# Attention and feed-forward kernel: moves of local results cut at multiples of 16 rows, V of most local blocks loaded in one transfer for all heads

## The chip, the cores and the metric

The kernel runs on one core of one Trainium2 chip. The metric is the device time of one execution in microseconds (us). The kernel before took 1079.87 us, the median of 3 runs (1079.04 to 1081.28).

## What is computed

Inputs q, k and v have 8 batches, 8 heads, 576 positions and 64 elements a head. Every head gets two attentions that are added: one over positions pooled by 4 (144 pooled positions, each result repeated 4 times), and a local one in which a position sees only positions less than 4 away. The result x (8 x 576 rows of 512) goes through a normalization and a feed-forward layer with a residual:

```
out_up    = repeat(softmax(q_d @ k_d.T * scale) @ v_d, 4)        # q_d, k_d, v_d: means of 4 positions
out_local = softmax(where(|i - j| < 4, q @ k.T * scale, -1e9)) @ v
x   = out_up + out_local                                          # as rows of 512 = 8 heads x 64
xn  = (x - mean(x)) / sqrt(var(x) + 1e-6) * g_ln
out = x + relu(xn @ w_ch1) @ w_ch2                                # 512 -> 2048 -> 512
```

## The kernel before, in words

All data are float32. The feed-forward products are made of three products of rounded parts each (`lo`, `hi` of the weights, `xh`, `xlo` and `hh`, `hl` of the data), and they are most of TensorE's work. The 4608 rows of x are 36 tiles of 128 rows (`x0` to `x35`), taken two at a time: 18 chunks c of 256 rows. For each chunk and each of 8 pairs p of weight columns, `up` (L996) makes `h`, ScalarE `relu` (L1003) makes `hh`, VectorE `rest` (L1007) makes `hl`, and `down` (L1019) adds into `acc`.

Local attention works on 40 windows (index i, 5 of them a batch). A window holds 116 positions as two blocks (`par`) of 58 results, read from 64 positions each. Windows 0 to 6 (`by_pe`) are turned by TensorE; in windows 7 to 39 q and k arrive as 32 x 32 blocks (`load_blocks`, L419, tiles `qr` and `kr`, 8 transfers each) and VectorE turns them (`turn`, L499). `load_v` (L437) brings V into one of four tiles `vwin`, with one partition half a block. The results of a window stand in `xl`, with the heads of a pair in different partition halves. `move` (L662) carries them by transfers within SBUF to the rows of x that they belong to: a block's 58 rows are one piece, or two where a tile of x ends within them, and each piece is two transfers, one for each head of the pairs.

The rest of a row's way: `load_up` (L865) reads the pooled result, GpSimd adds it to x (`plus`, L896), VectorE takes statistics (L904 to L907), GpSimd the inverse root (L910), VectorE normalizes (`xn`, L914), TensorE turns it (`px`, L923), ScalarE and VectorE split it (`xh` L930, `xlo` L940).

The order of every engine is set before the run by a planner (`Plan`, L23). Each piece of work is a task with an engine, a duration, the tasks it needs, a due time and the buffers it takes and gives. Most tiles come from one pool of 88 units (`u`). `xl` is one of them, and the task of a window's last move gives it back. A task that takes a unit may get one that the planner believes to be free from that time on. The planner lets a task end at its start and duration; its result is there a `lag` later. For the local blocks turned by VectorE the figures are:

```python
    DMA, LAT, W_AHEAD, W_LAG = 0.5, 2.5, 40, 1.5
        vt = add("SP", 2.65, load_v, (last_local.v[i % NVW],), due - 8.0, lag=LAT, kb=360, ahead=AHEAD)
            t = add("SP", 0.76 if by_pe else 1.52, move, outs, due + 1.0, take=() if n in piece else U,
                    give=U if e == len(moves) - 1 else (), lag=LAT, kb=116)
```

All loads, moves and stores are issued by SyncE (SP) in one queue, in the planner's order. Where a task waits on SP, all that stand behind it wait too. Between tasks of TensorE that the planner sees more than 0.4 us apart in the first 150 us of its plan, it puts spare matmuls (L197).

Of the kernel before, what the change touches and what calls it, by code (L numbers as in the profile page):

```python
# [22 lines left out]
class Plan:  # L23
# [14 lines left out]
    def add(self, eng, dur, fn, deps=(), due=0.0, take=(), give=(), lag=None, ahead=1e9, alt=None, kb=0):  # L38

        opts = {eng: (dur, fn, 0.0)}  # L40
        if alt is not None:
            opts[alt[0]] = alt[1:]
        t = SimpleNamespace(
            n=len(self.tasks), opts=opts, dur=dur, deps=[d for d in deps if d is not None],
            due=due, take=take, give=give, lag=lag, ahead=ahead, open=0.0, waits=0, eng=None, fn=None, kb=kb,
        )
        self.tasks.append(t)
        return t
# [91 lines left out]
def attention_then_ffn(  # L140
# [10 lines left out]
    nc = tc.nc  # L151

    P = 128
    B, H, S, D = q.shape
# [19 lines left out]
    NVW = 4  # L174
# [18 lines left out]
    def psa(name):  # L193
        p = ps_a.tile([P, 512], F32, tag="a", name=name)

        for _ in range(warm.pop() if warm else 0):
            nc.tensor.matmul(p[:, :P], lhsT=ident, rhs=ident, start=True, stop=True)  # L197
        return p
# [95 lines left out]
    def window_at(i):  # L294
        if NWIN <= i < NWIN + NEARLY:
            return w_base + i * w_gap - EARLY
        return w_base + i * w_gap if i >= NWIN else norm_at(0) - B0W - B0W_GAP * (2 - i)
# [7 lines left out]
    AHEAD = 45  # L305
# [14 lines left out]
    DMA, LAT, W_AHEAD, W_LAG = 0.5, 2.5, 40, 1.5  # L320
# [4 lines left out]
    def dve(n):  # L325
        return 0.06 + n / 950.0
# [72 lines left out]
    def window_start(w, par):  # L399
        return min(max(NQ * (2 * w + par) - (FACTOR - 1), 0), S - 64)  # L400

    chosen, own_moves = {}, []
    last_local = SimpleNamespace(v=[None] * NVW)

    def local(i):
        b, w = divmod(i, NWIN)
        due = window_at(i)
        add = plan.add
        x = SimpleNamespace(r={}, p={}, raw={})
        vwin = vwins[i % NVW]  # L410
# [21 lines left out]
        def load_v():  # L432
            for par in range(2):
                t0 = window_start(w, par)
                if not by_pe:
                    for h2 in range(2):
                        nc.sync.dma_start(  # L437
                            vwin[64 * par : 64 * par + 64, h2, :, :D],
                            v[b].rearrange("(p h) s d -> h s p d", h=2)[h2, t0 : t0 + 64],
                        )  # L440
                    continue
                for h2 in range(2):
                    nc.sync.dma_start(
                        vwin[64 * h2 : 64 * h2 + 64, par, :, :D],
                        v[b].rearrange("(p h) s d -> h s p d", h=2)[h2, t0 : t0 + 64],
                    )

        turned = []
        by_pe = i < NPE
        own = b < NPB  # L450
        for src, nm in ((q, "q"), (k, "k")):
            if by_pe:
# [15 lines left out]
                def sums(nm=nm):  # L468

                    for par in range(2):  # L470
# [17 lines left out]
                        lag=LAT, kb=360, ahead=AHEAD)  # L488
# [6 lines left out]
            else:  # L495
# [9 lines left out]
                for jb in range(2):  # L505
                    ts.append(add("SP", 4 * DMA, lambda src=src, nm=nm, jb=jb: load_blocks(src, nm, jb), ts,
                                  due - 14.0, take=() if jb else U, lag=LAT, kb=200, ahead=AHEAD))
                turned.append(add("DVE", dve(512), turn, ts, due - 8.0, take=U, give=U))
        vt = add("SP", 2.65, load_v, (last_local.v[i % NVW],), due - 8.0, lag=LAT, kb=360, ahead=AHEAD)

        def scores_by_pair():

# [71 lines left out]
        def times_v():  # L584


            x.pv = [
                psa(f"lv{i}_{n}")[:, : NPAIR * (D + 1)].rearrange("p (h e) -> p h e", h=NPAIR)
                for n in range(2)
            ]  # L590
            for pr in range(NPAIR):
                for n in range(2):
                    js = slice(64 * n, 64 * n + 64)
                    for m in range(2):
                        hs = slice(64 * m, 64 * m + 64)
                        nc.tensor.matmul(  # L596
                            x.pv[n][hs, pr], lhsT=x.at[js, pr, hs], rhs=vwin[js, m, pr], start=True, stop=True
                        )

        def inverse(h2):  # L600
# [24 lines left out]
        t = add("PE", 0.43, turn_a, (t,), due - 3.0, take=A, give=U)  # L625
        at = add("ACT", act(512), turn_a_out, (t,), due - 3.0, take=U, give=A)
        last_local.v[i % NVW] = tv = add("PE", 0.7, times_v, (at, vt), due - 1.0, take=(("a", 2),), give=U)
        outs = []
        for h2 in range(2):
# [6 lines left out]
        for par in range(2):  # L636
            s0 = NQ * (2 * w + par)
            n = min(NQ, S - s0)
            t, r0 = b * S + s0, s0 - window_start(w, par)
            while n:  # L640
                m = min(n, P - t % P)
                moves.append((t // P, t % P, r0, m, par))
                t, r0, n = t + m, r0 + m, n - m
        if own:
# [417 lines left out]
    for i in range(NPB * NWIN):  # L1062
        local(i)
    for b in range(B):
        pooled(b)
    for i in range(NPB * NWIN, B * NWIN):
        local(i)
# [48 lines left out]
```

## Time and profile before

| | kernel before |
|---|---|
| median of 3 runs | 1079.87 us (1079.04 to 1081.28) |
| profiled execution, span from first to last instruction | 1080.9 us |
| TensorE busy | 1040.3 us, 96% of the span |
| VectorE, ScalarE, GpSimd busy | 511.9, 312.7, 266.2 us |
| mean granted TensorE clock | 0.989 |
| bytes moved | 104.34 MB, mean 97 GB/s |

The profiled execution has no other time than its span; the span is 1.0 us above the median of the runs and within their range. TensorE is PE in the rows, VectorE DVE, ScalarE ACT, GpSimd POOL, SyncE's queue SPq; a `q` behind an engine's name is its sequencer. A busy time says that an engine had work, not that the work was at its fastest: at the lower of the clock's two levels the same matmul is busy longer.

### The profile page before, as it was taken

The page shows a single profiled execution, that of the slowest core. Times are in us where ns is not written, and L with a number is a line of the kernel's source. Part 1 is how long each engine was busy: PE and PEld are TensorE (multiplying, and loading weights), DVE is VectorE, ACT ScalarE, POOL GpSimd, SP SyncE. Part 2 cuts the span into 40 slices and gives each one's busy share as a digit, 9 for nine tenths or more (in the row PEclk, how much of TensorE's full clock was granted, in tenths as well). Part 3 has the DMA queues.
Part 4 walks back from the last instruction along what each step waited for, and adds up shares of the span by engine and source line. Part 5 has one row for each costly group of instructions (what it writes and reads, how often), then busy time and mean ns, then how long its engine had stood idle before and what let it go on. Part 6 is the DMA issues. An engine that isn't in the chain of part 4 may idle for free.

```text
span 1080.9 us, 23774 instructions
## 1 busy us (share of the span) xinstructions
PE 1040.3 (96%) x9290; PEld 933.6 (86%) x9290; DVE 511.9 (47%) x1309; ACT 312.7 (29%) x852; POOL 266.2 (25%) x285
## 2 busy tenths in 40 slices
PE   8987999989989999999999999999979999999998
PEld 8875898978879898989898989898968988888997
DVE  7699954434243535345344443645424353543211
ACT  5675633222222322132222221223212222222110
POOL 4234454314004221141213231142311400100000
PEclk9999899989999999999999999999999999999999
DMA  7798554625333443344343435252533333300000
GB/s 155 211 270 235 121 147 112 144 61 120 82 88 89 99 97 79 65 92 107 82 110 77 109 69 125 47 137 51 126 87 76 69 74 74 85 10 30 9 20 20
DMA packets 289296, 104.34 MB, mean 97 GB/s; under 512 B 237945, under 2 KB 276089, under 8 KB 289185
## 3 DMA queue, kind: packets, MB, share of 16 engines
q1 hardware_dynamic: 289185, 102.83, 40.2%
q8 instruction: 73, 1.20, 0.5%
q14 instruction: 38, 0.31, 0.1%
HBM read 82.58 MB, written 11.80 MB: 87 GB/s over the span
## 4 chain that ended last, share of the span: by engine, by line
PE 78%; DMA 9%; DVE 5%; SPq 4%; issue 2%; ACT 1%; POOL 1%; DVEq 0%; ACTq 0%; POOLq 0%
PE h L996 33%; PE acc L1019 32%; PE gv L802 3%; DMA s<-in_moe_w_ch_dram 2%; PE lv L596 2%; PE ls L540 2%; DMA x<-xl 2%; PE gs L766 2%; PE lt L575 1%; SPq L419 1%; PE px L923 1%; PE gt L785 1%; SPq L662 1%; DVE cva L370 1%; SPq L428 1%
## 5 line engine op out<-in xcount | busy, mean ns | idle before, releaser
L1019 PE MATMUL acc<-hi,hl 128*128 128x512 f32 x576 | 239.1, 415 | 10.2 <-DVE hl L1007 8.5
L1019 PE MATMUL acc<-lo,hh 128*128 128x512 f32 x576 | 228.5, 397 | 0.0
L1019 PE MATMUL acc<-hi,hh 128*128 128x512 f32 x576 | 226.8, 394 | 0.0
L1007 DVE SCALAR_TENSOR_TENSOR hl<-h,hh 128x512 fp32r<-128x512 f32 x144 | 98.9, 687 | 242.8 <-ACT hh L1003 222.8
L1003 ACT ACTIVATE hh<-h 128x512 fp32r<-128x512 f32 x144 | 86.1, 598 | 433.5 <-PE h L996 379.7
L996 PE MATMUL h<-xh,lo 128*128 128x256 f32 x1152 | 193.5, 290 | 0.0
L996 PE MATMUL h<-xlo,hi 128*128 128x256 f32 x1152 | 185.6, 284 | 0.0
L996 PE MATMUL h<-xh,hi 128*128 128x256 f32 x1152 | 185.6, 283 | 0.0
L996 PEld LDWEIGHTS h<-xh,lo 128*128 128x128 f32 x1152 | 169.4, 190 | 17.6 <-POOL lo L383 0.2
L996 PEld LDWEIGHTS h<-xlo,hi 128*128 128x128 f32 x1152 | 159.4, 192 | 0.0
L996 PEld LDWEIGHTS h<-xh,hi 128*128 128x128 f32 x1152 | 159.1, 192 | 0.0
L896 POOL TENSOR_TENSOR x<-x,up 128x512 f32<-128x512 f32 x32 | 41.2, 1289 | 376.8 <-DMA x<-xl 264.5
L1019 PEld LDWEIGHTS acc<-hi,hl 128*128 128x128 f32 x576 | 110.1, 191 | 27.5 <-DVE hl L1007 11.4
L1019 PEld LDWEIGHTS acc<-hi,hh 128*128 128x128 f32 x576 | 109.2, 190 | 25.3
L1019 PEld LDWEIGHTS acc<-lo,hh 128*128 128x128 f32 x576 | 110.3, 191 | 12.7
L930 ACT ACTIVATE xh<-px,gain 128x128 fp32r<-128x128 f32 x144 | 44.3, 367 | 79.5 <-PE px L923 43.6
L940 DVE SCALAR_TENSOR_TENSOR xlo<-px,gain,xh 128x128 fp32r<-128x128 f32 x144 | 43.0, 344 | 38.3 <-ACT xh L930 26.1
L904 DVE BATCH_NORM_STATS2 st<-x 128x6 f32<-128x512 f32 x32 | 22.1, 690 | 69.9 <-POOL x L896 68.7
L1027 DVE SCALAR_TENSOR_TENSOR x<-acc,x 128x512 f32<-128x512 f32 x36 | 24.3, 683 | 35.5 <-PE acc L1019 35.3
L546 DVE TENSOR_TENSOR ls<-ls,mask 128x256 f32<-128x256 f32 x66 | 27.0, 424 | 27.3 <-PE ls L540 22.3
L779 ACT ACTIVATE ag<-gs,gmx 96x144 f32<-96x144 f32 x96 | 28.8, 373 | 35.1 <-DVE gmx L771 33.1
L802 PEld LDWEIGHTS gv<-vd,agt 72*72 72x72 f32 x512 | 37.1, 145 | 1.5
(195 smaller groups left out, 1152.7 us busy)
## 6 DMA issues: line engine op xcount, KB each, us to landing
s<-in_moe_w_ch_dram SPq DMA_DIRECT2D x64, 256.0 KB
vwin<-in_v_dram SPq DMA_DIRECT2D x160, 64.0 KB
out_dram<-x SPq DMA_DIRECT2D x36, 256.0 KB
qr<-in_q_dram SPq DMA_DIRECT2D x264, 32.0 KB
kr<-in_k_dram SPq DMA_DIRECT2D x264, 32.0 KB
up<-ud SPq DMA_DIRECT2D x28, 256.0 KB
x<-xl SPq DMA_DIRECT2D x66, 58.0 KB
ud<-od SPq DMA_DIRECT2D x32, 72.0 KB
```

The lines of the kernel that those rows point to most:

```text
L546: nc.vector.tensor_add(x.ps[n], x.ps[n], mask.unsqueeze(1).broadcast_to([P, NPAIR, 64]))
L779: nc.scalar.activation(y.a[:, c], y.ps[:, c], AF.Exp, scale=POOLED_SCALE, bias=y.mx[:, c : c + 1])
L802: nc.tensor.matmul(y.pv[:, qh, h2], lhsT=y.at[kh][:, h2, qh * GH : (qh + 1) * GH], rhs=vd[:, kh, 2 * pr + h2], start=kh == 0, stop=kh == 1,)
L896: nc.gpsimd.tensor_add(xt[n], xt[n], x.up)
L904: nc.vector.bn_stats(st, x.up if by_pe else xt[n])
L930: nc.scalar.activation(xh[c][i][:, k, j * P : (j + 1) * P], pxt[n][:, kc], AF.Copy, scale=gain[:, kc : kc + 1])
L940: nc.vector.scalar_tensor_tensor(out=xlo[c][i][:, k, ts], in0=pxt[n][:, kc], scalar=gain[:, kc : kc + 1], in1=xh[c][i][:, k, ts].bitcast(F ...
L996: nc.tensor.matmul(ph[c, p][:, fi], lhsT=wt[:, kc], rhs=xx[kc // 2][:, kc % 2], start=n == 0, stop=n == 3 * KC - 1)
L1003: nc.scalar.activation(hh[c, p], ph[c, p], AF.Relu)
L1007: nc.vector.scalar_tensor_tensor(out=hl[c, p].rearrange("p c t -> p (c t)"), in0=ph[c, p].rearrange("p c t -> p (c t)"), scalar=0.0, in1=h ...
L1019: nc.tensor.matmul(acc[c][j], lhsT=lt[:, fi, ts], rhs=rt, start=p == 0 and fi == 0 and n == 0, stop=p == NPR - 1 and fi == 1 and n == 2,)
L1027: nc.vector.scalar_tensor_tensor(out=x, in0=acc[c][j], scalar=1.0 + 2.0**-23, in1=x, op0=ALU.mult, op1=ALU.add)
```

## The change

Two things. `load_v` of windows 7 to 39 issues one transfer per block for all 8 heads instead of one for each head of the pairs; so the tile is filled in the order of the heads, and `times_v` (L596) picks its part by another index. The planner's duration for it becomes 1.4 us. And the loop that lists the moves cuts a piece of m rows into the largest multiple of 16 rows and the remainder, for all windows (a remainder below 16 stays whole). Each cut piece is a task of its own with the durations above.

```diff
-                    for h2 in range(2):
-                        nc.sync.dma_start(
-                            vwin[64 * par : 64 * par + 64, h2, :, :D],
-                            v[b].rearrange("(p h) s d -> h s p d", h=2)[h2, t0 : t0 + 64],
-                        )
+                    nc.sync.dma_start(
+                        vwin.rearrange("p a b e -> p (a b) e")[64 * par : 64 * par + 64, :, :D],
+                        v[b, :, t0 : t0 + 64, :].rearrange("h s d -> s h d"),
+                    )
...
-        vt = add("SP", 2.65, load_v, (last_local.v[i % NVW],), due - 8.0, lag=LAT, kb=360, ahead=AHEAD)
+        vt = add("SP", 2.65 if by_pe else 1.4, load_v, (last_local.v[i % NVW],), due - 8.0, lag=LAT, kb=360, ahead=AHEAD)
...
-                            x.pv[n][hs, pr], lhsT=x.at[js, pr, hs], rhs=vwin[js, m, pr], start=True, stop=True
+                            x.pv[n][hs, pr], lhsT=x.at[js, pr, hs], rhs=vwin[js, m, pr] if by_pe else vwin[js, pr // 2, 2 * (pr % 2) + m], start=True, stop=True
...
                 m = min(n, P - t % P)
+                m = m // 16 * 16 or m
                 moves.append((t // P, t % P, r0, m, par))
```

In all, SyncE issues 1257 transfers instead of 1165: 94 loads of V instead of 160, and 350 moves instead of 192 (336 instead of 184 in windows 7 to 39). The planner then orders all engines anew. Three places follow; in the names the number behind a tile's name is its index, the last one a buffer's number, and `64x8x64 x2` means 64 partitions, 8 runs of 64 elements, two transfers in a row.

SyncE's queue at the moves of window 8 (`xl8`), with the loads of windows 10 and 11 (`qr`, `kr`) and of the pooled attention (`raw5`, `raw6`) around them. Before:

```order
L700 DMA raw5v1_3028<-in_v_dram 72x4x256
L419 DMA kr10_3034<-in_k_dram 32x8x32 x4
L419 DMA qr10_2969<-in_q_dram 32x8x32 x4
L825 DMA ud2_2687<-od4_1_3082 72x2x128
L419 DMA kr10_3034<-in_k_dram 32x8x32 x4
L700 DMA raw6q0_3140<-in_q_dram 72x4x256
L700 DMA raw6k0_3143<-in_k_dram 72x4x256
L662 DMA x7_2883<-xl8_3136 58x4x64 x2
L662 DMA x7_2883<-xl8_3136 42x4x64 x2
L662 DMA x8_3175<-xl8_3136 16x4x64 x2
```

Now:

```order
L419 DMA qr10_3004<-in_q_dram 32x8x32 x4
L700 DMA raw5v1_3132<-in_v_dram 72x4x256
L662 DMA x7_2919<-xl8_3128 48x4x64 x2
L662 DMA x7_2919<-xl8_3128 10x4x64 x2
L662 DMA x7_2919<-xl8_3128 32x4x64 x2
L662 DMA x7_2919<-xl8_3128 10x4x64 x2
L662 DMA x8_3200<-xl8_3128 16x4x64 x2
L700 DMA raw6q0_3217<-in_q_dram 72x4x256
L700 DMA raw6k0_3225<-in_k_dram 72x4x256
L436 DMA vwin0_76<-in_v_dram 64x8x64 x2
L419 DMA kr10_3252<-in_k_dram 32x8x32 x4
```

Between `raw5v1` and the moves stood 15 transfers; now there is none, and both halves of `kr10` come behind the moves.

SyncE's queue at the moves of window 31. Before:

```order
L865 DMA up27_10285<-ud6_9047 128x1x512
L419 DMA kr33_10232<-in_k_dram 32x8x32 x4
L437 DMA vwin3_79<-in_v_dram 64x4x64 x4
L662 DMA x27_10126<-xl31_10350 12x4x64 x2
L662 DMA x28_10378<-xl31_10350 46x4x64 x2
L662 DMA x28_10378<-xl31_10350 58x4x64 x2
```

Now:

```order
L865 DMA up27_10372<-ud6_9148 128x1x512
L419 DMA kr33_10392<-in_k_dram 32x8x32 x4
L419 DMA qr33_10367<-in_q_dram 32x8x32 x4
L662 DMA x27_10201<-xl31_10425 12x4x64 x2
L662 DMA x28_10453<-xl31_10425 32x4x64 x2
L662 DMA x28_10453<-xl31_10425 14x4x64 x2
L662 DMA x28_10453<-xl31_10425 48x4x64 x2
L662 DMA x28_10453<-xl31_10425 10x4x64 x2
L419 DMA kr33_10392<-in_k_dram 32x8x32 x4
L436 DMA vwin3_79<-in_v_dram 64x8x64 x2
```

The load of V and the second half of `kr33` have gone behind the moves, the second half of `qr33` stands just ahead of them; the moves are five pieces instead of three.

TensorE at the turn of tile 19 (`px19`), between the last products for chunk 8 (`h8_7` and `acc8`). Before:

```order
L996 MATMUL h8_7_7591<-xlo8_1_6940,hi1_15_2125 128x256 x2
L923 MATMUL px19_7639<-ident_66,xn19_7637 128x128 x4
L1019 MATMUL acc8_0_7240<-hi2_11_1876,hl8_5_7538 128x512
L1019 MATMUL acc8_0_7240<-lo2_11_1888,hh8_5_7505 128x512
L1019 MATMUL acc8_0_7240<-hi2_11_1876,hh8_5_7505 128x512
L1019 MATMUL acc8_1_7241<-hi2_11_1876,hl8_5_7538 128x512
L1019 MATMUL acc8_1_7241<-lo2_11_1888,hh8_5_7505 128x512
L1019 MATMUL acc8_1_7241<-hi2_11_1876,hh8_5_7505 128x512
L739 MATMUL gq10_1_7661<-ident_66,qd10_6945 128x72 x2
```

Now:

```order
L996 MATMUL h8_7_7650<-xlo8_1_6999,hi1_15_2149 128x256 x2
L1019 MATMUL acc8_0_7295<-hi2_11_1896,hl8_5_7595 128x512
L1019 MATMUL acc8_0_7295<-lo2_11_1919,hh8_5_7564 128x512
L1019 MATMUL acc8_0_7295<-hi2_11_1896,hh8_5_7564 128x512
L1019 MATMUL acc8_1_7296<-hi2_11_1896,hl8_5_7595 128x512
L1019 MATMUL acc8_1_7296<-lo2_11_1919,hh8_5_7564 128x512
L1019 MATMUL acc8_1_7296<-hi2_11_1896,hh8_5_7564 128x512
L923 MATMUL px19_7710<-ident_66,xn19_7706 128x128 x4
L739 MATMUL gq10_1_7719<-ident_66,qd10_6806 128x72 x2
```

Six products of `acc8` have gone ahead of `px19`. `px11` and `px29` have moved behind six products in the same way, and `lt9` (the turn of window 9's exponentials) behind six of `acc2`; around `px9` and `px27` the order on TensorE, VectorE and ScalarE is as before.

## Rows read from the trace of the kernel before

**Rows 1.** The page: span, and busy time of TensorE.
```profile
span 1080.9 us, 23774 instructions
PE 1040.3 (96%) x9290; PEld 933.6 (86%) x9290; DVE 511.9 (47%) x1309; ACT 312.7 (29%) x852; POOL 266.2 (25%) x285
```

**Rows 2.** TensorE's waits: line, releaser, total us, times, longest.
```profile
PE px L923 <- DVE xn L914: 13.3, 6, 5.8
```

**Rows 3.** Stretches of 27 us: busy us by engine, granted clock, DMA share, GB/s.
```profile
81.00:108.00 27.00, 19.14 (x166) 15.69 (x166) 26.31 (x47) 15.59 (x42) 13.44 (x11) 1.00 0.82 236
...
216.00:243.00 27.00, 22.01 (x182) 19.26 (x181) 9.26 (x23) 6.24 (x21) 4.24 (x5) 0.87 0.29 61
...
783.00:810.00 27.00, 21.30 (x165) 18.96 (x163) 6.54 (x20) 3.63 (x8) 3.06 (x3) 0.95 0.39 88
810.00:837.00 27.00, 26.92 (x231) 24.31 (x232) 12.79 (x34) 6.87 (x19) 2.77 (x3) 0.92 0.31 75
```

**Rows 4.** ScalarE in order of time at 808 us: start, duration, work, idle before.
```profile
808.30 0.62 ACT L930 ACTIVATE xh<-px,gain 128x128 fp32r<-128x128 f32 x2 [8.93 <-DMA x<-xl]
```

**Rows 5.** Chain that ended last: start, duration, what (three stretches).
```profile
575.55 4.91 DMA x<-xl
...
580.49 0.05 DVEq L940
...
784.53 1.78 DMA qr<-in_q_dram
...
802.83 5.25 DMA x<-xl
...
862.65 4.41 DMA x<-xl
```

**Rows 6.** TensorE's part of that chain: one `down` of two `acc` tiles.
```profile
570.91 1.39 PE acc L1019 x6
```

**Rows 7.** SyncE's queue in order of time, before the moves of window 31.
```profile
793.03 2.06 SPq L419 DMA_DIRECT2D kr<-in_k_dram  x4
795.22 3.14 SPq L437 DMA_DIRECT2D vwin<-in_v_dram  x4
798.46 5.99 SPq L662 DMA_DIRECT2D x<-xl  x6
```

**Rows 8.** SyncE, window 18's second move of 58 rows, and the next one.
```profile
478.19 0.79 SPq L662 DMA_DIRECT2D x<-xl  x1
479.08 1.59 SPq L662 DMA_DIRECT2D x<-xl  x1
```

**Rows 9.** Moves of window 34 (48, then 10 rows), and GpSimd behind them.
```profile
887.00 0.60 SPq L662 DMA_DIRECT2D x<-xl  x1
887.72 0.86 SPq L662 DMA_DIRECT2D x<-xl  x1
889.18 1.30 POOL L896 TENSOR_TENSOR x<-x,up 128x512 f32<-128x512 f32 x1 [24.56 <-DMA x<-xl]
```

**Rows 10.** Issue times of SyncE's lines: count, ns min/median/max, first and last start.
```profile
L662 SPq DMA_DIRECT2D x<-xl x184: 605/787/2176, 194.5 to 1001.6; - x184
L437 SPq DMA_DIRECT2D vwin<-in_v_dram x132: 595/615/1601, 98.5 to 907.7; - x132
L428 SPq DMA_DIRECT2D qn<-in_q_dram x14: 596/634/1471, 1.3 to 53.7; - x14
```

**Rows 11.** SyncE's queue in order of time, at the moves of window 8.
```profile
211.43 2.71 SPq L419 DMA_DIRECT2D kr<-in_k_dram  x4
...
219.49 7.91 SPq L662 DMA_DIRECT2D x<-xl  x6
```

**Rows 12.** VectorE's last work for `xl8`.
```profile
213.47 0.41 DVE L612 TENSOR_TENSOR xl<-lv,lr 128x256 f32<-128x256 f32 x1
```

**Rows 13.** GpSimd's step of the chain behind the moves of window 8.
```profile
227.73 1.30 POOL x L896
```

**Rows 14.** SyncE's waits: line, releaser, total us, times, longest.
```profile
SPq L1033 <- DVE x L1027: 90.1, 16, 38.2
```

## Prediction

> **What bounds the kernel now.** I read the page first: TensorE is busy for 1040.3 of 1080.9 us [rows 1]. Neither part of the change touches a matmul's size or number, apart from a few spare ones, so at most the 40.6 idle us can be won, and what the lower clock costs. Then the waits of TensorE and the stretches of 27 us, to see where the idle time lies. It is not spread. In the first 135 us VectorE is the limit: from 81 to 108 us it is busy for 26.31 of 27 us, and TensorE idles for 7.9 [rows 3]. After 200 us nearly all idle time is a wait of `px` for `xn`: 13.3 us in six waits, the longest 5.8 [rows 2], and one of the six, a short one, lies before 200 us. One more stop, at 230 us, has 27 - 22.01 = 5.0 us [rows 3]. Behind the two long stops the granted clock is below 1: 0.87 from 216 to 243, 0.95 and 0.92 from 783 to 837 us [rows 3]; the clock has two levels, 2.4 and 1.2 GHz, and a mean below 1 is time at the lower. That costs about 27 x 0.13 = 3.5 and 27 x (0.05 + 0.08) = 3.5 us. So 13.3 + 5.0 + 7.0 = 25.3 us are all that can be won outside the start.
>
> The chain of waits tells what stands behind these stops: moves of 58 rows. At 804 us TensorE waits for `px27`, VectorE for an `xlo` ahead of `xn27`, and ScalarE has stood idle for 8.93 us because its `xh` needs a unit that a move still reads; the last of window 31's moves was issued at 802.83 and landed 5.25 us later, and `xh` ran at 808.30 [rows 4, 5]. At 581 us VectorE's own `xlo` waits in the same way for a move that took 4.91, at 867 us for one that took 4.41 [rows 5]. At 230 us it is the sum itself: GpSimd begins `x7` at 227.73, though `xl8` was ready at 213.9 [rows 12, 13].
>
> In all of them the planner was wrong by about the same. It counts 1.52 us for a piece and 2.5 us until it has landed. Window 31's three pieces should take 3 x 1.52 + 2.5 = 7.1 us from the first issue to the last landing; they took from 798.46 to 808.08, 9.6 us [rows 5, 7]. So units were given away, and work was queued, 2.5 us too early.
>
> **The moves.** Two transfers of 58 rows hold up what is issued next: 0.79 us for the second, 1.59 for the one behind it, where 0.79 is usual [rows 8, 10]. A transfer of 48 rows takes 0.60 us to issue, and GpSimd starts on its data 889.18 - 887.00 = 2.2 us after its issue began [rows 9]; a 10-row one takes 0.86 to issue. So a 58-row piece goes from 2 x 0.79 + 0.8 of hold-up to 0.60 x 2 + 0.86 x 2, with a gap of 0.05 behind each: 2.5 before, 3.1 now. What becomes shorter is only the end: 2.2 instead of 4.4 to 5.25 us behind the last issue.
>
> The Trainium skill, in "DMA: Bandwidth & Descriptors" (section "Why a DMA increments its semaphore by 16 and not by 1"), says that a transfer uses as many of 16 engines as the largest number up to 16 that divides its slowest dimension: 2 for 58 rows, 16 for 48, 10 for 10. The trace agrees, as far as it has such rows: 4.4 to 5.25 us against 2.2. By bytes alone 48 rows would take 48/58 of 4.4, or 3.6 us, and the end would gain 0.8 instead of 2 us or more.
>
> Other cuts gain nothing there and only add issues. There are 336 transfers instead of 184 in windows 7 to 39, 10.2 a window instead of 5.6. At the mean of 0.60 and 0.86 with the gap, 0.78, a window takes 7.9 us; window 31 took 5.99 with six and I take 5.6 for the mean [rows 7]. That is +2.3 us a window. For window 31 (12, 32, 14, 48, 10) the last landing is 9 issues x 0.78 + 2.2 = 9.2 us after the first issue, against 9.6. With six pieces, as in 13 windows, it is 11 x 0.78 + 2.2 = 10.8, later than that.
>
> So the moves do not become faster on the whole. But the planner now counts 5 x 1.52 + 2.5 = 10.1 us for what should take 9.2, where it had counted 7.1 for 9.6. It errs to the safe side, and its new order shows it.
>
> **V.** 132 transfers become 66 with the same bytes. Four issues of 0.615 and their gaps are 2.7 us; two, of 0.634 as the loads of `qn` with the same shape take [rows 10], are 1.4: -1.3 us a window. The planner's figures agree with both. The products with V read as many rows as before, from another place of the tile: no cost; I take 0 and at worst 0.1 us a window.
>
> SyncE so issues for 2.3 - 1.3 = 1.0 us more per window, 33 us in all. From below this costs nothing: SyncE waits for the results' stores alone for 90.1 us, 38.2 of it at the end [rows 14]. From above it costs all 33.
>
> **Place by place,** from the new order:
> - 230 us. The moves of window 8 stood behind 15 transfers, issued from 211.43 to 219.49 [rows 11]. Now none stands between `raw5v1` and them, and `xl8` is ready at 213.88 [rows 12]. So they start up to 5.6 us earlier and last as long (9 x 0.78 against 7.9). `lt9`, which waited, also stands behind six products of 1.39 us in all more. The stop and its clock go: 5.0 + 3.5 = 8.5.
> - 804 us. The load of V (3.14 us) and half of `kr33` (2.06) have gone behind the moves [rows 7], so they may start 5.2 us earlier. But `up27`, which must wait for `ud6`, may not come earlier, and behind it there is now half of `qr33` in V's place: then it is 1.1 us. Add 0.4 from the moves themselves; of the stop's 5.8 us I take 4, and the clock's 3.5: 7.5.
> - `px19`, `px11` and `px29` stand behind six products, 1.39 us [rows 6], or two such groups; `px9` has its moves ahead of V. These are the rest of the 13.3: 7.5 us, and I take 7.
>
> The sum is 23.0 us. New stops come against it. Before, six of 33 windows led to one, at 25.3 / 6 = 4.2 us with the clock. The queue is fuller and later loads now stand behind the moves; with errors on the safe side I take half as many, three: +12.6. Its bounds are 0 and 33. At the start the moves of window 5 and some loads for the pooled attention now stand ahead of weights on SyncE, and some `hl` ahead of conversions of weights on VectorE: both signs, I take +0.5, from -4 to +6 (half of the 7.9 idle us [rows 3], or most of it again). So -23.0 + 12.6 + 0.5 = -9.9, and 1080.9 - 9.9 = 1071.0 for the profiled execution; it is 1.0 above the median of the runs, so 1070.0.
>
> **Rivals.**
> 1. *Loads come late instead (slower).* Half of k now stands behind the moves (`kr10`, `kr33`). A block lands about 1.8 us after its issue [rows 5]; behind five pieces (7.8 us) the last of four is issued 9.3 us after the first move and lands 11 us after it. VectorE turns it in a fixed place, and the `xlo` and `hl` behind it wait. Without its stop VectorE would be at `lkt33` some 3 us after the `xh` of [rows 4] less 5.8, at about 805.5 by estimate; so it decides against us where the moves start later than 794.5, and every such window then stops TensorE by the excess. With all 33 us of added issue exposed, against 23 won, it gives 1080 + 10 = 1090. For it: the queue's length; against it: the planner knows the new durations and moved these loads itself.
>
> The Trainium skill speaks for it in the same page ("Rules for kernel authors"): small transfers are mostly overhead and belong together, and here 58 KB become 48 and 10. The trace agrees for the issue: a tenth of the bytes takes 0.86 us.
>
> 2. *The stops only change places.* As many windows as before have one, at other tiles, 23 against 23: 1080. For it: the buffers are as scarce as before, and six-piece windows land later. Against it: the common error of 2.5 us is gone.
>
> 3. *All goes, and the start too.* No new stop, and 4 us at the start: 1079.9 - 23 - 4 = 1053. Against it: the fuller queue, and that the start's limit, VectorE, gets no less to do.
>
> 4. *Cutting does not help a transfer* (48 rows land as 58 do). Then the planner's 2.5 us are short again, with more pieces: 1080 or more. Rows 9 speak against it: 2.2 us. I give it 2%, within rival 2.
>
> **How the numbers follow.** The forecast, most stops gone and a few new ones, 0.57, at 1070, its own range 1060 to 1078; rival 1 0.20; rival 2 0.15; rival 3 0.08. A measurement of this kernel can tell 0.2%, 2.2 us, from no change. Faster by more: nearly all of the forecast (0.55), rival 3 (0.08) and a little of rival 2 (0.02): 0.65. Slower: rival 1 (0.19) and a quarter of rival 2: 0.23. The rest, 0.12, is the same. The range that leaves out 2 in 10 runs from 1056, near rival 3, to 1087, near rival 1.
>
> **What would show it.** Right: the moves of 48 rows issue in 0.6 to 0.7 us, the second of 58 rows no longer delays the next, no `xh` or `xlo` waits for a move, the wait of `px` for `xn` falls below 6 us, and the clock stays at 1 after 200 us. Wrong: `px` waits as long at other tiles; or VectorE's L499 waits for loads of k and TensorE for `hl`; or the start, up to 135 us, has more than 5 us of idle time added. If SyncE's issue time grows by well over 40 us, the moves were under-priced.

## The result, and the profile after

The changed kernel takes 1069.38 us, the median of 4 runs (1068.29 to 1071.13), against 1079.72 (1079.04 to 1081.28) for the one before: a ratio of 0.9898, with a 95% interval of 0.9883 to 0.9913. The forecast was 1070.0. The two profiled executions lie further apart than the medians, 1067.7 and 1080.9 us of span, so that what follows has 13.2 us to explain, of which 10.3 are the change and the rest is the choice of executions: in every run that has both, the device time is 1.7 to 2.3 us above the span, so the profiled execution of before was not 1.0 but some 3 us slower than its median.

The page of the changed kernel, its span and the engines' busy times:

```profile
span 1067.7 us, 24014 instructions
PE 1043.4 (98%) x9318; PEld 937.9 (88%) x9318; DVE 509.0 (48%) x1304; ACT 317.7 (30%) x872; POOL 266.5 (25%) x285
```

TensorE's idle time fell from 40.6 [rows 1] to 24.3 us. Its waits now (line, releaser, total us, times, longest), in which the line of [rows 2] no longer stands at all:

```profile
PE acc L1019 <- DVE hl L1007: 4.6, 3, 2.3
PE gs L766 <- ACT ktg L752: 3.5, 2, 2.8
PE lv L595 <- ACT at L581: 2.7, 1, 2.7
PE lk L457 <- DMA kn<-in_k_dram: 2.5, 2, 1.6
...
PE gv L802 <- POOL mv L910: 1.6, 1, 1.6
```

The stretches of [rows 3] after 200 us, of the changed kernel (TensorE's busy time first, then weight loads, VectorE, ScalarE, GpSimd, granted clock, DMA share, GB/s). From 216 to 243 us the stop and the low clock are gone; the second place still has 2.8 idle us:

```profile
216.00:243.00 27.00, 26.30 (x228) 23.37 (x227) 14.17 (x35) 8.05 (x28) 10.95 (x11) 1.00 0.55 104
...
783.00:810.00 27.00, 24.21 (x176) 21.66 (x174) 8.56 (x21) 6.42 (x20) 3.10 (x3) 0.94 0.39 83
810.00:837.00 27.00, 27.00 (x256) 24.54 (x246) 14.68 (x36) 6.32 (x16) 10.13 (x11) 1.00 0.28 77
```

The same from 200 to 1062 us, of the kernel before:

```profile
200.00:1062.00 862.00, 844.33 (x7465) 758.73 (x7465) 359.48 (x941) 206.18 (x559) 180.83 (x186) 0.99 0.35 80
```

and of the changed kernel; 17.7 idle us became 3.5:

```profile
200.00:1062.00 862.00, 858.51 (x7608) 772.75 (x7604) 359.94 (x943) 215.51 (x592) 183.29 (x188) 1.00 0.37 81
```

Fixed stretches do not hold the same work in both kernels. A mark that stands at the same point of the feed-forward work in both is the n-th `hh` (one for each chunk and pair, 144 in all). These are the 20th and the 24th on ScalarE in order of time (start, duration), of the kernel before:

```profile
210.20 0.60 ACT L1003 ACTIVATE hh<-h 128x512 fp32r<-128x512 f32 x1 [1.93 <-DMA vwin<-in_v_dram]
...
245.36 0.60 ACT L1003 ACTIVATE hh<-h 128x512 fp32r<-128x512 f32 x1 [0.81 <-PE h L996]
```

and of the changed kernel:

```profile
215.18 0.60 ACT L1003 ACTIVATE hh<-h 128x512 fp32r<-128x512 f32 x1 [1.92 <-PE h L996]
...
244.32 0.60 ACT L1003 ACTIVATE hh<-h 128x512 fp32r<-128x512 f32 x1
```

So the changed kernel is 5.0 us behind at the 20th, 1.0 ahead at the 24th, past the first stop, and at the last it is 13.1 ahead (1057.2 against 1070.3): in this pair of executions it wins 18.1 us after the start and loses 5.0 in it.

SyncE, moves of window 18 one by one (48, 48, 10, 10 rows), answering [rows 8]; none of the four is held up:

```profile
469.95 0.64 SPq L662 DMA_DIRECT2D x<-xl  x1
470.64 0.63 SPq L662 DMA_DIRECT2D x<-xl  x1
471.32 0.82 SPq L662 DMA_DIRECT2D x<-xl  x1
472.18 0.79 SPq L662 DMA_DIRECT2D x<-xl  x1
```

At window 31, VectorE's last work for `xl31`, of the kernel before:

```profile
790.16 0.73 DVE L612 TENSOR_TENSOR xl<-lv,lr 128x256 f32<-128x256 f32 x2
```

of the changed kernel:

```profile
782.89 0.73 DVE L611 TENSOR_TENSOR xl<-lv,lr 128x256 f32<-128x256 f32 x2
```

and SyncE's queue of the changed kernel at that place, answering [rows 7]:

```profile
784.99 1.93 SPq L419 DMA_DIRECT2D qr<-in_q_dram  x4
787.01 7.95 SPq L662 DMA_DIRECT2D x<-xl  x10
795.01 2.96 SPq L419 DMA_DIRECT2D kr<-in_k_dram  x4
798.01 1.40 SPq L436 DMA_DIRECT2D vwin<-in_v_dram  x2
```

Before, the moves began 798.46 - 790.89 = 7.6 us after their data were ready; now 787.01 - 783.62 = 3.4. They hold the queue for 7.95 us instead of 5.99, and V for 1.40.

The stop that is left at this place is a new one. The chain that ended last, of the changed kernel, shows it (start, us, what):

```profile
796.02 1.46 SPq L419
...
797.52 1.97 DMA kr<-in_k_dram
...
799.61 0.06 DVE lkt L498
...
800.25 0.58 DVE xlo L940 x2
...
800.85 0.62 ACT xh L930 x2
...
802.25 1.26 PE gs L766 x6
```

The last part of `kr33`, now behind the moves, was issued 10.5 us after the first of them, since the part ahead of it took 1.46 us to issue where the others took 0.44 to 0.47, and landed at 799.49; VectorE waited for it to turn it, with `xlo` behind; `xh`, `ktg` and TensorE's `gs` waited in turn.

### The profile page after: what moved, and what is told of

The parts are those of the page before. It is cut to its first block, busy times and chain, and to the rows that moved or that the text cites. A ratio compares the mean times of both kernels' runs of the same rounds, so it can differ in the third digit from the quotient of the medians.

```text
span 1067.7 us, 24014 instructions
## 1 busy us (share of the span) xinstructions
PE 1043.4 (98%) x9318; PEld 937.9 (88%) x9318; DVE 509.0 (48%) x1304; ACT 317.7 (30%) x872; POOL 266.5 (25%) x285
## 4 chain that ended last, share of the span: by engine, by line
PE 74%; SPq 1%; DMA 1%; DVE 1%; issue 0%; ACT 0%; POOL 0%; POOLq 0%; DVEq 0%
PE h L996 32%; PE acc L1019 31%; PE gv L802 2%; PE lv L595 2%; PE ls L539 2%; PE gs L766 2%; PE lt L574 1%; PE px L923 1%; PE gt L785 1%; SPq L419 1%; SPq L662 1%; DMA kr<-in_k_dram 1%; PE gq L739 0%; DMA x<-xl 0%; DVE x L1027 0%
## 5 line engine op out<-in xcount | busy, mean ns | idle before, releaser
L1019 PEld LDWEIGHTS acc<-lo,hh 128*128 128x128 f32 x576 | 110.0, 191 | 12.6
L802 PE MATMUL gv<-vd,agt 72*72 72x65 f32 x512 | 37.9, 228 | 1.6 <-POOL mv L910 1.6
L910 POOL TENSOR_TENSOR mv<-mv,neg_half 128x1 f32<-128x1 f32 x36 | 19.8, 549 | 77.8 <-DVE mv L907 67.0
```

The source lines that it names most:

```text
L802: nc.tensor.matmul(y.pv[:, qh, h2], lhsT=y.at[kh][:, h2, qh * GH : (qh + 1) * GH], rhs=vd[:, kh, 2 * pr + h2], start=kh == 0, stop=kh == 1,)
L1019: nc.tensor.matmul(acc[c][j], lhsT=lt[:, fi, ts], rhs=rt, start=p == 0 and fi == 0 and n == 0, stop=p == NPR - 1 and fi == 1 and n == 2,)
```

## The experiments

Theory A: the stops came from moves whose hold on SyncE's queue and whose landing the planner counted too short, and they went because the figures now fit. Theory B: they went because the transfers themselves got better. Theory C: any new order is a draw, and this one was a good one. The first four runs take the change apart: each part alone, and the order apart from the transfers. All ratios are against the kernel before, run beside each, with 95% intervals. The diffs show the lines that matter, not always the whole edit; the words beside them say the rest.

**V alone** (`e1_v`): the change without the line that cuts moves.

```diff
                 m = min(n, P - t % P)
-                m = m // 16 * 16 or m
                 moves.append((t // P, t % P, r0, m, par))
```

> Only V: one transfer per block for all heads, planned at 1.4 us; the moves stay uncut and the planner's figures for them stay. Theory A (the stops before came from moves that the planner counted about 2.5 us too short, and went because its figures now fit): those figures are unchanged, so the stops stay, if at other tiles; 1075 to 1081 us, and px still waits for xn for 8 us or more. Theory B (the transfers themselves got better: SyncE's queue is shorter by V's 44 us): 1072 to 1076. Theory C (any new order is as good as a draw, +-10 us around 1075): anywhere from 1068 to 1085.

Measured: 1076.27 us, 0.9960 (0.9943 to 0.9977). `px` waited for `xn` for 7.9 us. About 4 us come with V and its order together; this run does not separate the two.

**Moves alone** (`e2_moves`): that line put into the kernel before.

```diff
                 m = min(n, P - t % P)
+                m = m // 16 * 16 or m
```

> Only the moves: cut at multiples of 16 rows, each piece planned with 1.52 us; V as before. Theory A: nearly all of the gain, 1068 to 1073 us, px waits for xn for under 4 us although SyncE issues for some 65 us more than before. Theory B: the longer queue without V's saving eats the gain, 1076 to 1084. Theory C: anywhere from 1068 to 1085.

Measured: 1073.22 us, 0.9924 (0.9902 to 0.9946); `px` waits for `xn` once, 2.8 us. Most of the gain, though the issue times on SyncE's queue add up to 744 us where they were 672 before: against B's figure. The sum of both parts, 0.4 and 0.8%, is about the whole.

**The old order with the new transfers** (`e3_oldorder`): the planner lists the uncut moves and V at 2.65 us, so all engines keep the order of before; at its turn a move issues the cut transfers, and V is one transfer.

```diff
-                to = xt[n][p0 : p0 + m]
+                for o, k in cuts(m):          # (0, m // 16 * 16) and the remainder
+                    to, r = xt[n][p0 + o : p0 + o + k], r0 + o
```

> The planner sees the kernel before, so the order of all engines is that of before; but each move is issued as the cut transfers, and V of the blocks turned by VectorE as one transfer. Theory A: most of the stops stay, since the last landing of a window is hardly earlier and their place in the order is the old one; V ahead of window 31's moves gives 2 us there: 1074 to 1081. Theory B: the faster landing takes the stops away, 1067 to 1072. Theory C says nothing against either.

Measured: 1078.65 us, 0.9978 (0.9956 to 0.9999). The stops stay where they were, some shorter and one longer. TensorE's waits of that run:

```profile
PE lt L578 <- ACT la L573: 7.7, 2, 6.6
PE px L927 <- DVE xn L918: 6.5, 5, 2.4
```

**The new order with the old transfers** (`e4_neworder`): the tasks of the changed kernel, but the first part's task issues the whole piece and the remainder's issues nothing; V in four transfers, planned at 1.4.

```diff
+                f = min(n, P - t % P)
+                m = f // 16 * 16 or f
+                moves.append((t // P, t % P, r0, f, par))
+                if f > m:
+                    moves.append((t // P, t % P + m, r0 + m, 0, par))
```

> The planner sees the changed kernel, so the order of all engines is the changed one; but the transfers are those of before: a piece of 58 rows goes whole at the task of its first part and the task of the remainder issues nothing, V goes in four transfers. Theory A: nearly the whole gain, 1068 to 1073 us. Theory B: the stops at landings of 58 rows come back, 1077 to 1083. Theory C: as theory A, since the order is the lucky one.

Measured: 1069.67 us, 0.9899 (0.9874 to 0.9925): the time of the changed kernel with none of its transfers. Theory B has fallen as the main cause: the run before this one leaves the transfers at most 0.4%. The order makes the gain; A and C are left.

**The new order, V in one transfer, moves uncut** (`e11_newv_oldmoves`): the run above with the new `load_v`.

```diff
+                    nc.sync.dma_start(
+                        vwin.rearrange("p a b e -> p (a b) e")[64 * par : 64 * par + 64, :, :D],
+                        v[b, :, t0 : t0 + 64, :].rearrange("h s d -> s h d"),
+                    )
```

> The order of the changed kernel, the moves uncut as before (as in the run with the new order and the old transfers), but V in one transfer per block. SyncE issues for about 44 us less than in that run and for some 70 less than in the changed kernel. Theory A: the order sets the time; at most 2 us are won, 1066 to 1070. Theory B (SyncE's queue still matters): 1060 to 1065.

Measured: 1066.23 us, 0.9880 (0.9840 to 0.9921). After 200 us its longest wait is 0.4 us. Its waits of `px` for `xn`:

```profile
PE px L927 <- DVE xn L918: 0.6, 2, 0.4
```

With V in four transfers (the run before this one) the same order had one long stop there:

```profile
PE px L928 <- DVE xn L919: 5.8, 2, 5.2
```

**Measured figures for 58 rows** (`e5_honest`): the kernel before, with two of the planner's numbers changed and not one transfer.

```diff
-            t = add("SP", 0.76 if by_pe else 1.52, move, outs, due + 1.0, take=() if n in piece else U,
-                    give=U if e == len(moves) - 1 else (), lag=LAT, kb=116)
+            t = add("SP", 0.76 if by_pe else 2.4 if m == NQ else 1.52, move, outs, due + 1.0, take=() if n in piece else U,
+                    give=U if e == len(moves) - 1 else (), lag=3.6 if m == NQ and not by_pe else LAT, kb=116)
```

> The kernel before with its own transfers; only the planner's figures for a move of 58 rows become what the trace of before showed: 2.4 us instead of 1.52 for its two issues and the hold-up of the next, and 3.6 us instead of 2.5 until it has landed. Theory A (figures too short made the stops): most stops go, 1069 to 1075 us, and px waits for xn for under 5 us. Theory C (the changed order was a lucky draw): a slightly different order, anywhere from 1070 to 1086, most likely near 1079.

Measured: 1067.44 us, 0.9888 (0.9854 to 0.9923). All of the change's gain, with neither of its parts, and more than theory A had expected.

**The landing alone** (`e6_lag`), 1.52 us kept:

```diff
-                    give=U if e == len(moves) - 1 else (), lag=LAT, kb=116)
+                    give=U if e == len(moves) - 1 else (), lag=5.0 if m == NQ and not by_pe else LAT, kb=116)
```

> The kernel before with its own transfers and durations; only the time until a move of 58 rows has landed becomes 5.0 us in the planner instead of 2.5. It tells whether the landing alone matters, which decides when xl's unit counts as free, or the length of SyncE's queue too. Theory A by the landing: as e5, 1069 to 1075 us. Theory A by the queue: 1076 to 1080. Theory C: anywhere from 1070 to 1086.

Measured: 1081.88 us, 1.0017 (0.9998 to 1.0036). No gain: a longer time until the landing, without the longer hold, changes nothing.

**The duration alone** (`e12_dur`), the lag kept:

```diff
-            t = add("SP", 0.76 if by_pe else 1.52, move, outs, due + 1.0, take=() if n in piece else U,
+            t = add("SP", 0.76 if by_pe else 2.4 if m == NQ else 1.52, move, outs, due + 1.0, take=() if n in piece else U,
```

> The kernel before with its own transfers; only the planner's duration for a move of 58 rows is 2.4 us instead of 1.52, the time until it has landed stays 2.5. Theory A1 (what the planner had wrong is how long SyncE's queue is held): the gain of the run with both figures, 1065 to 1071 us. Theory A2 (both figures are needed): 1073 to 1080. Theory C (draws): anywhere from 1066 to 1083.

Measured: 1072.31 us, 0.9925 (0.9892 to 0.9957), between the ranges of A1 and A2. Most or all of the gain; the interval meets that of both figures together, so whether the lag adds something on top stays open. `px` waited for 6.2 us there, in five waits of at most 2.4.

What the duration does can be read in SyncE's queue. VectorE's end of `xl31` in the run with the landing alone:

```profile
787.80 0.72 DVE L612 TENSOR_TENSOR xl<-lv,lr 128x256 f32<-128x256 f32 x2
```

SyncE's queue there, to the first move of window 31:

```profile
793.16 2.06 SPq L419 DMA_DIRECT2D kr<-in_k_dram  x4
795.32 2.65 SPq L437 DMA_DIRECT2D vwin<-in_v_dram  x4
798.06 0.89 SPq L662 DMA_DIRECT2D x<-xl  x1
```

VectorE's end of `xl31` in the run with the duration alone:

```profile
780.55 0.76 DVE L612 TENSOR_TENSOR xl<-lv,lr 128x256 f32<-128x256 f32 x2
```

and SyncE's queue there:

```profile
782.24 0.55 SPq L865 DMA_DIRECT2D up<-ud  x1
782.89 2.64 SPq L437 DMA_DIRECT2D vwin<-in_v_dram  x4
785.62 5.99 SPq L662 DMA_DIRECT2D x<-xl  x6
791.71 5.09 SPq L419 DMA_DIRECT2D kr<-in_k_dram  x8
```

The moves begin 9.5 us after their data in the first and 4.3 in the second, where the load of k has gone behind them. A planner that thinks the queue is emptier than it is puts loads ahead of a move, in a gap that is not there; told a longer hold, it here lets the move go first.

At window 8, the stop at 230 us, the same shift works otherwise. The kernel before has the loads `raw6q` and `raw6k` just ahead of the moves; in the run with the duration alone they stand behind. VectorE's end of `xl8` and SyncE's queue of that run:

```profile
212.98 0.42 DVE L612 TENSOR_TENSOR xl<-lv,lr 128x256 f32<-128x256 f32 x1
...
218.55 5.54 SPq L662 DMA_DIRECT2D x<-xl  x6
224.19 0.49 SPq L700 DMA_DIRECT2D raw6q<-in_q_dram  x1
```

The moves begin hardly earlier, 5.2 us after their data against 5.6 [rows 11, 12], but the same six transfers take 5.54 us instead of 7.91: the second of them takes 0.79 us to issue instead of 2.18. `lt` waits 0.4 us there instead of 5.0. These are two places, each in one profile; the other stops were not followed in this way.

Theory C is tested by more draws: orders changed by a figure that means nothing.

**The changed kernel with 1.50 instead of 1.52 us** (`e8_new150`), **the measured figures with 2.5 instead of 2.4** (`e14_honest_redraw`), and **the kernel before with 1.56 instead of 1.52** (`e9_old156`), all in the same line; the diff is that of the third:

```diff
-            t = add("SP", 0.76 if by_pe else 1.52, move, outs, due + 1.0, take=() if n in piece else U,
+            t = add("SP", 0.76 if by_pe else 1.56, move, outs, due + 1.0, take=() if n in piece else U,
```

> The changed kernel with another figure that means nothing: 1.50 instead of 1.52 us for a piece in the planner, which gives another order with the same safe side (a piece takes 1.3 to 1.7 us). Theory A: the gain stays within a few us, 1066 to 1074. Theory C: a new draw, 1068 to 1085, with the middle near 1077.

Measured: 1069.08 us, 0.9901 (0.9866 to 0.9937).

> As the run with both figures as measured, but 2.5 us instead of 2.4: another order from figures that are as good. Theory A: 1065 to 1071 us. Theory C: a new draw, 1066 to 1083.

Measured: 1066.87 us, 0.9867 (0.9847 to 0.9887), the lowest ratio, if not clear of the others' intervals.

> The kernel before with a figure that means nothing: 1.56 instead of 1.52 us for a piece. Another order, with the move of 58 rows still counted too short. Theory A: the stops stay, 1075 to 1083 us. Theory C: a new draw, 1066 to 1083.

Measured: 1082.62 us, 1.0014 (0.9993 to 1.0034). The stops stay; the largest sum of waits is again that of `px`:

```profile
PE px L923 <- DVE xn L914: 10.6, 5, 5.1
```

**Measured figures and V in one transfer** (`e13_honest_v`): both diffs above on the kernel before, V planned at 1.4 us.

> V in one transfer, planned at 1.4 us; moves uncut; the planner's figures for 58 rows as measured (2.4 us, landed 3.6 us later). Theories A1 and A2: the gain of the run with both figures and SyncE's queue 44 us shorter: 1062 to 1068 us, the fastest of all or level with it. Theory C: anywhere from 1064 to 1082.

Measured: 1069.21 us, 0.9892 (0.9863 to 0.9920): SyncE's shorter queue gave nothing measurable on top of the measured figures, against what theory A had expected (1062 to 1068).

Together: nine kernels (seven different orders) in which the planner counts more time on the queue for the moves of 58 rows, be it by pieces or by the figure, lie between 0.9867 and 0.9925. Three in which it does not, and V is planned as before (`e6_lag`, `e9_old156`, and `e3_oldorder` with the very order of before), lie between 0.9978 and 1.0017. `e1_v`, with V planned anew and the moves as before, lies between the groups. The profiles divide in the same way where the start is left out: from the 20th `hh` to the last, the nine take 837 to 846 us, the three and the kernel before 857 to 861, `e1_v` 852. `e12_dur` and `e9_old156` even have the same order on TensorE, by operations and tile names, and lie 10 us apart: what divides them is the order on SyncE and the engines that feed TensorE. A draw would hardly divide so, and C has fallen as the main cause; that the nine differ by up to 6 us among each other may be what remains of it. The orders are not far from each other, so this is no statement on all orders. One rival was not tried: more time counted than measured, or counted at other tasks of SyncE. So it is shown that more time for these moves makes the gain, not that the measured figure is the best one.

## Why the prediction was right, and where it was not

- *What can be won.* The stops after 200 us and the clock behind them, 25.3 us by the forecast, were the right place: idle time there fell by 14.2 us, and the clock there is low only once, 0.94 in one stretch (27 x 0.06 = 1.6 us against 7.0).
- *The moves do not get faster, the order does it.* Right, and shown by the runs with one order and the other's transfers: 0.9978 and 0.9899. The issue of window 31's ten transfers was forecast at 7.8 us and took 7.95; V 1.4 and took 1.40.
- *Why the planner was wrong.* Half right. The forecast put the 2.5 us down to issue and landing together and said that units were given away too early. The landing counted 2.5 us longer, which gives `xl`'s unit back later in the 12 windows whose last piece has 58 rows, window 31 among them, changed nothing (1.0017); the hold on the queue, 0.8 to 0.9 us for each piece of 58 rows, was enough for 0.9925. The wait of `xh` for a unit at 804 us [rows 4] was real, but the move that held it was late because it had stood 7.6 us in the queue.
- *Place by place.* 230 us: gone with its clock, as forecast. `px19`, `px11`, `px29`, `px9`: gone. 804 us: `px27` no longer waits, but 2.8 us came back as another stop. It is rival 1 in small, at the place that the forecast named: the second half of `kr33` was expected 11 us after the first move and landed 12.5 us after it. It decided one window and not all 33. (In that rival's argument from the size of transfers, 10 rows are about a sixth of the bytes of 58, not a tenth.)
- *New stops.* Forecast 12.6 us; measured 3.5 idle and 1.6 of the clock after 200 us, 5.1. This term was sized too large.
- *The start.* Forecast +0.5 (-4 to +6), measured +5.0 at the 20th `hh` in these two profiles. It was sized too small for them. Idle time is not the reason: up to 135 us it fell from 17.2 to 13.9 us. Between 60 and 135 us the granted clock was 0.91 against 0.93 and from 135 to 200 us 0.97 against 1.00, and `gv` waited 1.6 us for GpSimd's `mv`. Besides, the planner put 32 spare matmuls between 146 and 156 us, where the kernel before has none; they are 3.6 us of TensorE that count as busy, and the forecast had put them at nothing. Whether the order costs this is open: `e4_neworder`, with the same order, was at its 20th `hh` at 210.50, as early as the kernel before, with the same spare matmuls and a clock of 0.98 from 60 to 135 us; `e11_newv_oldmoves`, again with the same order, at 215.75, with 0.89.
- *The signs that were named.* `px` no longer waits for `xn`, the moves of 48 rows issue in 0.63 us (median of 92), and SyncE's issue times grew by 24 us without the gaps, from 672 to 696, where 33 with the gaps were forecast. Two signs came only in part: `xh` still waited for a move, once and for 2.3 us (before 13.3, in two waits), and `xlo` once for 1.5 (before 6.7, in two); and the clock was not 1 throughout.

The stretches of the start, of the kernel before (TensorE's busy time first; the granted clock is the third number from the end):

```profile
60.00:135.00 75.00, 61.38 (x465) 54.09 (x465) 70.17 (x128) 46.18 (x122) 32.94 (x27) 0.93 0.74 202
135.00:200.00 65.00, 63.04 (x549) 57.24 (x549) 35.84 (x84) 21.51 (x64) 31.25 (x30) 1.00 0.51 123
```

and of the changed kernel:

```profile
60.00:135.00 75.00, 63.98 (x482) 56.31 (x481) 68.98 (x127) 43.79 (x115) 32.84 (x27) 0.91 0.74 202
135.00:200.00 65.00, 61.81 (x505) 56.05 (x507) 35.28 (x80) 20.80 (x60) 29.15 (x28) 0.97 0.51 117
```

The rows of these spare matmuls, of the changed kernel after 133 us (count, shortest, median and longest ns, first and last start):

```profile
L197 PE MATMUL gv<-ident x14: 275/275/302, 154.0 to 155.5; 128*128 128x128 f32 x14
L197 PE MATMUL gt<-ident x10: 272/275/275, 152.4 to 153.4; 128*128 128x128 f32 x10
L197 PE MATMUL gq<-ident x8: 272/275/275, 146.2 to 147.0; 128*128 128x128 f32 x8
```

The two mis-sized terms have opposite signs, 7.5 too much and 4.5 too little, and the profiled pair came out 3.3 us below the forecast for it (a span of 1067.7 against 1071.0). That the median came within 0.6 us of its forecast is more luck than the sum deserves. Rival 4, that cutting does not help a transfer, turned out not to matter: the order won without any cut.

## What to carry to other kernels

Where a planner sets the order, an operation that holds a queue longer than the planner counts can show up elsewhere, here as loads put ahead of something that was already due. Measure how long each kind of operation holds its issuing queue, including what it does to the next one, and correct the figure first; here two numbers gave the whole gain of a change to the transfers. And to learn what a change does, run its order with the old operations, and the old order with its operations.

## What was not expected

Shorter and better spread transfers, in the old order, made the stop at 230 us longer, not shorter: `lt` waited 6.6 us, where before TensorE had been idle for 5.0 [rows 3]. The moves did not hold the queue longer there; they began 1.1 us later than before, and took 7.60 us for 7.91 [rows 11]. SyncE's queue of that run:

```profile
220.59 7.60 SPq L666 DMA_DIRECT2D x<-xl  x10
```

GpSimd began `x7` at 228.22, 0.5 us later than before [rows 13], and TensorE came to the place earlier: it was 1.1 us ahead at the 20th `hh` (209.09 against 210.20). Together that is the 1.6 us by which the wait grew. So the longer wait says nothing against the transfers; it is one profile of each.
